# An attention-and-MLP kernel: ScalarE's evacuation of the product with V moves behind the exponential and the high half of its step

## The chip, the core and the metric

The kernel runs on one NeuronCore of a Trainium2 chip. The metric is the device time of one execution in microseconds (us); three runs of the kernel before gave 865.6, 866.25 and 870.39, so the median is 866.25. Engines are called as the profile calls them: PE is TensorE (PEld its weight loads), DVE VectorE, ACT ScalarE, POOL GpSimd, SP SyncE, whose queue issues most of the DMAs.

## What is computed

Attention over 4 batches with 8 heads each, with queries averaged in pairs, followed by a layer norm and a two-layer MLP that is added to its input:

```python
batch, n_heads, seq, head_dim = (4, 8, 1152, 64)
q_pool = q.reshape(B, H, S // factor, factor, D).mean(axis=3)
scores = scale * np.matmul(q_pool, k.transpose(0, 1, 3, 2))
scores = scores - np.max(scores, axis=-1, keepdims=True)
attn = np.exp(scores)
attn = attn / (np.sum(attn, axis=-1, keepdims=True) + 1e-09)
x = heads of np.matmul(attn, v) side by side          # (4, 576, 512)
xn = (x - mu) / np.sqrt(var + 1e-06) * g_ln
out = x + np.maximum(xn @ w_ch1, 0.0) @ w_ch2         # 512 -> 2048 -> 512
```

## The kernel before

The attention is cut into 144 steps. A step is one block of 128 query rows of one pair of heads against all 1152 keys; nine steps make a pair of heads, 36 steps a batch. Products that need more than half precision are made from high and low fp16 halves. The program is one long list written by `step(i)`, and each engine executes its own part of that list strictly in order; nothing reorders it later.

From the second batch on (steps 36 to 143) a step goes through these stations, named by their lines:

- PE writes the scores of step i+1 to PSUM (L362 for the first 1024 keys, L370 for the last 128). The scores of a step fill a slot of three PSUM banks; even and odd steps use two slots in turn. Scores take only the first 128 columns of the slot's third bank, and columns 128 to 257 of that bank hold the product with V of an earlier step.
- DVE finds the row maximum (L381, `mx`) and scales it (L386, `nb`). ACT computes the exponential (L395, `pe`) and its fp16 high half (L409, `hl`). DVE, or in three steps of nine POOL (L251, L416), makes the low half (L418), and SP issues the DMA that transposes both halves (L421, `pt`). Three `hl` buffers are in turn.
- Four steps later PE multiplies the transposed block with V (`emit_pv`, L464, 27 short accumulations in a row); this is called a piece. Its evacuation has two parts (`evac_pv`): `one` on DVE adds a small number to the row sums and inverts them (L513, L514, `r`), `two` on ACT scales the 64 result columns by `r` into `xb` (L524; `xh` for the fifth step of a pair, as two instructions).
- `evacuated` then counts, and when the eight heads of 128 rows are complete it queues a layer norm: DVE takes statistics (L550, L551), POOL normalizes (L556 to L562), PE transposes (L568).
- Between the steps PE runs units of the MLP (L605 the first layer, L637 the second), as a rule one per step, and preparations of the next pair (L297, L301, L325 transposes of k and q). A unit or preparation takes one of two remaining PSUM banks, and must be evacuated before the bank is written again: units by ACT L618 and DVE L619 (`ht`) or DVE L650, preparations by ACT L286 or L311 and DVE L283 or L306. ACT also computes sums of absolute values for the scales of a pair (L185), which PE transposes (L201).

The order around the change: evacuations are collected in the list `evacs`, in the order of their matmuls: first the piece, then the unit, then the preparation, all of them issued at the end of step i-1. `flush()` in step i runs the list: it stands after the scores of step i+1, behind the maximum of step i on DVE and ahead of the exponential of step i on ACT. A unit can also call `flush()` in its middle, so that in some steps the list runs at the step's end.

Of the kernel before, what the change touches and what calls it, by code (L numbers as in the profile page):

```python
# [24 lines left out]
def tile_pooled_attention_moe(  # L25
# [310 lines left out]
    def on_pe(i):  # L336

        return 0 <= i < HP * C
# [67 lines left out]
    def emit_hi(i):  # L406
        st = steps[i]
        hl = st["hl"] = p_p.tile([128, 2, S], FP16, tag="hl", name="hl", bufs=3)
        nc.scalar.activation(out=hl[:, 0], in_=st["pe"], func=ACTF.Copy, scale=2.0 ** 15)  # L409
# [21 lines left out]
    def emit_t_copy(i):  # L431
        st = steps[i]
        for a, b in ((0, 512), (512, S)):
            nc.scalar.copy(st["pt"][:, a:b], st["s"][:, a:b])

    def emit_pv(i, ps=None):

        p, j = divmod(i, C)
        b, hp = divmod(p, HP)
        vt, pt = pair[p]["v"], pts.pop(i)  # L440
        if ps is None:
            ps = psum[:, 3 * (pv_slot[0] % 2) + 2, 128:258]
        if j == 4:
            o = 64 * (b % 2)
            parts = [(h, 64 * h, 64, ps[o:o + 64, 65 * h:65 * h + 65]) for h in range(2)]
        else:
            parts = [(PLACES[p % HP // 2][j][0], 0, 128, ps[:, 0:65])]
        if on_pe(i):
            pt = pt.rearrange("p a n -> p (a n)").bitcast(FP32)
            for h, q0, w, _ in parts:  # L450
                for u, c in enumerate(ORDER):
                    nc.tensor.matmul(  # L452
                        out=ps[0:65, q0:q0 + w], lhsT=vt[:, h, c],
                        rhs=pt[:, 128 * u + q0:128 * u + q0 + w],
                        start=(u == 0), stop=(u == C - 1),
                    )
            return ps
        for h, q0, w, dst in parts:
            for u, c in enumerate(ORDER):
                x = vt[:, h, c]  # L460
                hi, lo = pt[:, u, q0:q0 + w], pt[:, C + u, q0:q0 + w]
                for lhsT, rhs in ((hi, x[:, 0:65]), (hi, x[:, 66:130]), (lo, x[:, 0:65])):
                    n = rhs.shape[1]
                    nc.tensor.matmul(  # L464
                        out=dst[:, 0:n], lhsT=lhsT, rhs=rhs,
                        start=(u == 0 and lhsT is hi and n == 65),
                        stop=(u == C - 1 and lhsT is lo),
                        skip_group_check=True,
                    )
        return ps  # L470
# [16 lines left out]
    def evac_pv(i, ps):  # L487

        p, j = divmod(i, C)
        b, hp = divmod(p, HP)  # L490
        s = pair[p]["s"][:, 2:3]
        r = sm_p.tile([128, 2], FP32, tag="r", name="r", bufs=3)
        if j == 4:
            if b % 2 == 0 and hp == 0:
                xh[b // 2] = x_p.tile([128, 2, DM], FP32, tag="hh", name="xh")
            o, n, m = 64 * (b % 2), 64, 2
            x = xh[b // 2][o:o + n, 0, 128 * hp:128 * hp + 128]
        else:
            if j == 0 and hp == 0:
                room["x"] -= 4  # L500
                assert room["x"] >= 0
                xb[b] = x_p.tile([128, 4, DM], FP32, tag="xb", name="xb")
            h, t = PLACES[hp // 2][j]
            o, n, m = 0, 128, 1
            x = xb[b][:, t, 128 * hp + 64 * h:128 * hp + 64 * h + 64]
        r = r[o:o + n, 0:m]

        def one():
            sums = ps[o:o + n, 64:65 * m:65]
            if on_pe(i):  # L510
                nc.vector.reciprocal(r, sums)
            else:
                nc.vector.tensor_scalar(r, sums, EPS, s[o:o + n], op0=ALU.add, op1=ALU.mult)  # L513
                nc.vector.reciprocal(r, r)  # L514

        def two():
            for u in range(m):
                if on_pe(i):
                    nc.vector.tensor_scalar(
                        x[:, 64 * u:64 * u + 64], ps[o:o + n, 65 * u:65 * u + 64],  # L520
                        r[:, u:u + 1], None, op0=ALU.mult,
                    )
                    continue
                nc.scalar.activation(  # L524
                    out=x[:, 64 * u:64 * u + 64], in_=ps[o:o + n, 65 * u:65 * u + 64],
                    func=ACTF.Copy, scale=r[:, u:u + 1],
                )

        return one, two
# [7 lines left out]
    def bank():  # L537
        for _ in range(2):
            for _ in free_banks:
                nbank[0] += 1  # L540
                n = nbank[1] = free_banks[nbank[0] % len(free_banks)]
                if n not in held and n not in waiting:
                    waiting.add(n)
                    return psum[:, n]
            flush()
# [31 lines left out]


    units, preps = deque(), deque()
    evacs = []  # L580

    def flush():
        mine, evacs[:] = list(evacs), []
# [333 lines left out]
    def evacuated(n):  # L917

        p, j = divmod(n, C)
        b = p // HP  # L920
        left[p] -= 1
        if not left[p]:
            pair.pop(p)
        key = ("h", b // 2) if j == 4 else (b, PLACES[p % HP // 2][j][1])
        whole[key] = whole.get(key, 0) + 1
        if whole[key] == 8 and key != ("h", 0):
            norms.append(key)
# [7 lines left out]
    def a_prep():  # L935
        if preps:
            fn, p, u = preps.popleft()
            evacs.extend(fn(p, u))
# [6 lines left out]
    def a_piece(i):  # L945
        pieces.extend(ready.pop(i, ()))
        for u in range(2 if len(pieces) > 2 and not on_pe(i) else 1):
            if pieces:
                n = pieces.popleft()
                pt = pts[n]  # L950
                ps = emit_pv(n, bank() if u or on_pe(n) else None)
                if on_pe(n):
                    ot = pt.rearrange("p a n -> p (a n)").bitcast(FP32)[0:65, 0:128]
                    evacs.append(lambda ot=ot, ps=ps: nc.scalar.activation(
                        out=ot, in_=ps[0:65, 0:128], func=ACTF.Identity, bias=eps
                    ))
                    turned.append((n, ot))
                    continue
                evacs.extend(evac_pv(n, ps))
                evacs.append(lambda n=n: evacuated(n))  # L960

    def step(i):
        live = i < NSTEP
        this[0] = i
        for fn, a in early.pop(i, ()):
            fn(*a)
        if live:
            emit_max(i)
        if on_pe(i - 1):
            emit_t_copy(i - 1)  # L970
            steps.pop(i - 1)
        while found:
            found.popleft()()
        first = on_pe(i - 2) or on_pe(i)
        if first and not on_pe(i):
            a_piece(i)
        if on_pe(i):
            if i < 3:
                warm(16, bank())
            a_piece(i)  # L980
            a_prep()
            emit_exp(i)
        while scaled_out:
            scaled_out.popleft()()
        if i + 1 < NSTEP:
            emit_s(i + 1)
            pv_slot[0] = i + 1
        else:
            free_banks[:] = [6, 7, 0, 1, 3, 4]
            pv_slot[0] += 1  # L990
        if on_pe(i):
            while fill:
                drip()
            flush()
        else:
            flush()
            if live:
                emit_exp(i)
                emit_hi(i)
        if 0 <= i - 1 < NSTEP and not on_pe(i - 1):  # L1000
            emit_lo(i - 1)
            steps.pop(i - 1)
            drip()
        norm(i)
        while soon or len(fill) > 3:
            drip()
        if on_pe(i):
            emit_t(i)
            if reds:
                found.append(reds.popleft()())  # L1010
        elif reds:
            evacs.append(reds.popleft()())
        while turned:
            n, ot = turned.popleft()
            emit_turn(n, ot, i)
        if not on_pe(i):
            if not first:
                a_piece(i)
            some_units(i)
            a_prep()  # L1020
        for fn, a in todo.pop(i, ()):
            fn(*a)
        if calm and i < HP * C - 1:
            gate()
        for _ in range(1 if i < HP * C - 1 else 2):
            if calm:
                fn, n = calm.popleft()
                fn(n)
# [6 lines left out]
    with tc.manual_schedule():  # L1035
# [33 lines left out]
        one, two = all_max(st["acc"], 3, lambda ps: scales(0, ps, 0, 3, both=True))  # L1069
# [46 lines left out]
```

## Time and profile before

| | us |
|---|---|
| median of 3 runs | 866.25 |
| the profiled execution, its own time | 860.85 |
| its span on the core | 859.0 |
| PE busy in the span | 810.0 (94%) |
| DVE busy | 604.2 (70%) |
| ACT busy | 561.8 (65%) |
| POOL busy | 349.5 (41%) |

The program has three stages. The first batch takes the time up to about 183 us and treats its pieces in another way (PE transposes them, and DVE scales them in L519, which reads the same 64 columns of the third bank as L524 does later). The second to fourth batch take from 183 to about 735 us. From 735 us to the end the attention is over and PE works off the remaining units. Busy times are shares of the span; the time of an engine between two of its instructions is idle time, and the profile names the event that ended it. Idle time of an engine that is not the bound costs nothing by itself.

### The profile page before, as it was taken

The numbers are of one execution on the slowest core, as the hardware profiler recorded it, in microseconds if no ns is written. First come the engines' busy times: TensorE is split into PE (matmuls) and PEld (weight loads), VectorE is DVE, ScalarE is ACT, GpSimd is POOL, SyncE is SP. The second block draws the span as 40 slices with busy tenths as digits, with TensorE's granted clock in tenths as the row PEclk, the third lists the DMA queues.
The fourth block names the chain that finished last, engine by engine and source line by source line (L and its number), as shares of the span: only waits on it lengthen the run. The fifth ranks groups of instructions, "written<-read, shape, count | busy, mean of one in ns | idle before, by whom it ended". The sixth has DMA issues, their size and how long they took to land.

```text
span 859.0 us, 21617 instructions
## 1 busy us (share of the span) xinstructions
PE 810.0 (94%) x9142; PEld 574.4 (67%) x9142; DVE 604.2 (70%) x1166; ACT 561.8 (65%) x810; POOL 349.5 (41%) x345
## 2 busy tenths in 40 slices
PE   7999999988889998998999999999999999999997
PEld 6787877766556665656575766666666666766764
DVE  4698899898778877788777777777777777531221
ACT  3999988867676767677686867676867676311110
POOL 3020333487888845436534244634542514300000
PEclk9999999999999999999999999999999999999999
DMA  6853465025695869887898989776989968500001
GB/s 178 223 206 122 158 179 182 1 63 107 134 203 110 175 124 223 147 166 141 156 180 158 174 146 203 146 153 123 217 143 158 171 117 139 100 10 20 19 2 24
DMA packets 276016, 115.95 MB, mean 135 GB/s; under 512 B 259280, under 2 KB 259280, under 8 KB 275920
## 3 DMA queue, kind: packets, MB, share of 16 engines
q1 hardware_dynamic: 275568, 113.70, 64.5%
q8 instruction: 71, 1.16, 0.6%
q10 hardware_dynamic: 352, 0.88, 0.4%
q14 instruction: 25, 0.20, 0.1%
HBM read 46.14 MB, written 4.72 MB: 59 GB/s over the span
## 4 chain that ended last, share of the span: by engine, by line
PE 45%; DVE 27%; ACT 12%; DMA 8%; issue 4%; POOL 2%; SPq 2%; ACTq 0%; POOLq 0%; DVEq 0%
PE psum L637 14%; PE psum L605 14%; DVE mx L381 8%; DVE hl L418 6%; PE psum L464 5%; PE psum L362 4%; ACT pe L395 3%; DMA qr<-in_q_dram 2%; DMA kr<-in_k_dram 2%; DVE ht L619 2%; PE psum L452 2%; ACT ht L618 2%; DMA pt<-hl 2%; DVE kt L283 2%; PE psum L428 2%
## 5 line engine op out<-in xcount | busy, mean ns | idle before, releaser
L381 DVE TENSOR_REDUCE mx<-psum 128x1 f32<-128x1152 f32 x144 | 194.7, 1352 | 19.3 <-ACT xb L524 7.4
L637 PE MATMUL psum<-wsl,ht 128*128 128x512 f16 x864 | 196.6, 379 | 5.1 <-DVE ht L619 4.3
L395 ACT ACTIVATE pe<-psum,nb,sc 128x1152 f32<-128x1152 f32 x144 | 188.8, 1311 | 11.8 <-DVE nb L386 10.4
L605 PEld LDWEIGHTS <-wsl 128*128 128x128 f16 x1920 | 170.2, 98 | 28.2 <-issue 9.6
L605 PE MATMUL psum<-xn,wsl 128*128 128x256 f16 x1536 | 178.1, 274 | 8.8 <-DVE xb L650 5.9
L637 PEld LDWEIGHTS <-ht 128*128 128x128 f16 x864 | 80.8, 98 | 93.6 <-issue 5.8
L409 ACT ACTIVATE hl<-pe 128x1152 f16<-128x1152 f32 x108 | 125.6, 1163 | 9.5 <-DMA pt<-hl 6.2
L362 PE MATMUL psum<-kt,qt 64*128 64x512 f16 (+1 forms) x960 | 127.3, 380 | 1.9 <-ACT pe L395 0.9
L619 DVE SCALAR_TENSOR_TENSOR ht<-psum,ht 128x512 f16<-128x512 f32 x72 | 49.8, 692 | 100.7 <-ACT ht L618 100.7
L464 PE MATMUL psum<-vt,pt 128*128 128x65 f16 (+1 forms) x3240 | 118.4, 194 | 0.2 <-DMA pt<-hl 0.2
L418 DVE SCALAR_TENSOR_TENSOR hl<-pe,hl 128x1152 f16<-128x1152 f32 x72 | 112.1, 1556 | 0.0
L464 PEld LDWEIGHTS <-pt 128*128 128x128 f16 (+1 forms) x3240 | 110.1, 101 | 2.8 <-DMA pt<-hl 0.7
L618 ACT ACTIVATE ht<-psum 128x512 f16<-128x512 f32 x72 | 42.7, 593 | 87.0 <-PE psum L605 86.6
L251 POOL TENSOR_SCALAR pe<-pe 128x1152 f32<-128x1152 f32 x36 | 43.1, 1198 | 130.5 <-ACT hl L409 130.5
L524 ACT ACTIVATE xb<-psum,r 128x64 f32<-128x64 f32 x96 | 29.9, 311 | 93.8 <-DVE r L514 80.6
L416 POOL TENSOR_TENSOR hl<-pe,hl 128x1152 f16<-128x1152 f32 x36 | 85.5, 2374 | 3.0
L452 PE MATMUL psum<-pt,vt 128*65 128x128 f32 (+1 forms) x720 | 77.4, 263 | 1.1 <-DVE qt L283 1.1
L452 PEld LDWEIGHTS psum<-pt,vt 128*65 128x65 f32 x720 | 71.5, 138 | 1.3 <-DVE qt L283 1.3
L362 PEld LDWEIGHTS <-qt 64*128 64x128 f16 (+1 forms) x960 | 39.7, 96 | 39.6 <-issue 22.1
L370 PEld LDWEIGHTS <-qt 128*128 128x128 f16 (+1 forms) x320 | 17.0, 99 | 61.5 <-issue 61.4
L283 DVE SCALAR_TENSOR_TENSOR qt<-psum,s,qt 128x384 f16<-128x384 f32 x48 | 29.5, 615 | 31.1 <-ACT qt L286 31.0
L257 POOL COPY gate<-gate 128x1 f32<-128x1 f32 x27 | 5.2, 193 | 110.5 <-DVE gate L256 110.5
(116 smaller groups left out, 1010.8 us busy)
## 6 DMA issues: line engine op xcount, KB each, us to landing
stage<-in_moe_w_ch_dram SPq DMA_DIRECT2D x32, 512.0 KB, 5.9
kr<-in_k_dram SPq DMA_DIRECT2D x16, 576.0 KB, 4.6
qr<-in_q_dram SPq DMA_DIRECT2D x31, 288.0 KB, 6.1
vr<-in_v_dram SPq DMA_DIRECT2D x15, 576.0 KB, 5.0
out_dram<-xb SPq DMA_DIRECT2D x32, 128.0 KB, 2.4
pt<-hl SPq DMA_TRANSPOSE x108, 4.9
kr<-in_k_dram SPq DMA_DIRECT2D x16, 64.0 KB, 4.2
vr<-in_v_dram ACTq DMA_DIRECT2D x1, 576.0 KB, 6.5
```

What stands on the lines that cost most here:

```text
L362: nc.tensor.matmul(out=sp[o:o + w, c0:c0 + 512], lhsT=qt[r:r + 64, qa, q0:q0 + w], rhs=kt[r:r + 64, ka, h], start=(a == 0), stop=(a == 2),)
L381: nc.vector.tensor_reduce(mx, st["s"], axis=AX.X, op=ALU.max)
L395: nc.scalar.activation(out=st["pe"], in_=st["s"], func=ACTF.Exp, scale=pair[i // C]["sc"][:, 0:1], bias=st["nb"],)
L409: nc.scalar.activation(out=hl[:, 0], in_=st["pe"], func=ACTF.Copy, scale=2.0 ** 15)
L416: nc.gpsimd.tensor_tensor(hl[:, 1], st["pe"], hl[:, 0], op=ALU.subtract)
L418: nc.vector.scalar_tensor_tensor(hl[:, 1], st["pe"], 2.0 ** 15, hl[:, 0], op0=ALU.mult, op1=ALU.subtract)
L452: nc.tensor.matmul(out=ps[0:65, q0:q0 + w], lhsT=vt[:, h, c], rhs=pt[:, 128 * u + q0:128 * u + q0 + w], start=(u == 0), stop=(u == C - 1),)
L464: nc.tensor.matmul(out=dst[:, 0:n], lhsT=lhsT, rhs=rhs, start=(u == 0 and lhsT is hi and n == 65), stop=(u == C - 1 and lhsT is lo), skip_ ...
L605: nc.tensor.matmul(out=ps[:, o:o + n], lhsT=wsl[:, 8 * w + cc, wa, f * 128:f * 128 + 128], rhs=xn[:, xa * KD + cc, 0:n], start=(m == 0), s ...
L618: lambda: nc.scalar.activation(out=hi, in_=pv, func=ACTF.Relu),
L619: lambda: nc.vector.scalar_tensor_tensor(lo, pv, 0.0, hi, op0=ALU.max, op1=ALU.subtract),
L637: nc.tensor.matmul(out=ps, lhsT=hv[0][:, ha, f, t * 128:t * 128 + 128], rhs=wsl[:, 8 * w + 4 + f // 2, wa, (f % 2) * DM:(f % 2) * DM + DM] ...
```

## The change

`evac_pv` still returns `one` and `two`, but only `one` goes to `evacs`. `two` and the call of `evacuated` go to a new list, `last`. A step takes what is in `last` when it starts, and runs it behind the exponential and the high half of that step.

```diff
-    evacs = []
+    evacs, last = [], []
...
-                evacs.extend(evac_pv(n, ps))
-                evacs.append(lambda n=n: evacuated(n))
+                one, two = evac_pv(n, ps)
+                evacs.append(one)
+                last.extend((two, lambda n=n: evacuated(n)))
...
         first = on_pe(i - 2) or on_pe(i)
+        final, last[:] = list(last), []
...
             if live:
                 emit_exp(i)
                 emit_hi(i)
+        for fn in final:
+            fn()
```

On ACT, step 60 (about 309 to 314 us in the trace of before), the last rows of step 59 ahead of it. In before:

```order
L395 ACTIVATE pe_4325<-psum_79,nb_4302,sc_3313 128x1152
L409 ACTIVATE hl_4327<-pe_4325 128x1152
L524 ACTIVATE xb_2799<-psum_79,r_4359 128x64
L618 ACTIVATE ht_4100<-psum_79 128x512
L311 ACTIVATE kt_4045<-psum_79,s_4043 128x256
L395 ACTIVATE pe_4410<-psum_79,nb_4392,sc_3313 128x1152
L409 ACTIVATE hl_4412<-pe_4410 128x1152
L524 ACTIVATE xb_2799<-psum_79,r_4445 128x64
```

The same place in the changed kernel:

```order
L395 ACTIVATE pe_4324<-psum_79,nb_4302,sc_3313 128x1152
L409 ACTIVATE hl_4326<-pe_4324 128x1152
L524 ACTIVATE xb_2799<-psum_79,r_4271 128x64
L618 ACTIVATE ht_4100<-psum_79 128x512
L311 ACTIVATE kt_4045<-psum_79,s_4043 128x256
L395 ACTIVATE pe_4409<-psum_79,nb_4392,sc_3313 128x1152
L409 ACTIVATE hl_4411<-pe_4409 128x1152
L524 ACTIVATE xb_2799<-psum_79,r_4359 128x64
```

The kinds of rows stand in the same sequence; what moved is which piece L524 evacuates: `r_4359`, which DVE makes in step 60 after that step's maximum, stands ahead of L618 in before and behind L409 now, and in its old place stands `r_4271` of the step ahead.

On PE, at the scores of a step of the later batches (last score matmuls, as a piece of the difference, with the semaphores waited for):

```order
 L362 MATMUL psum<-kt,qt 128x512
 L370 LDWEIGHTS qt
-L370 MATMUL psum<-kt,qt 128x128
+L370 MATMUL psum<-kt,qt 128x128 [waits Activation_49]
 L370 LDWEIGHTS qt
 L370 MATMUL psum<-kt,qt 128x128
```

No PE row moved; the first matmul into the third bank of a slot now waits for the L524 that last read that bank. This is so in 101 steps; before, it waited for DVE's L513 or for nothing of its own.

On DVE, at the statistics of a layer norm (the step that begins at 390 us in the trace of before):

```order
 L619 SCALAR_TENSOR_TENSOR ht<-psum,ht 128x512 [waits Activation_49]
 L418 SCALAR_TENSOR_TENSOR hl<-pe,hl 128x1152 [waits DMAHW5_49]
-L550 BN_STATS bs<-xb 128x6
+L550 BN_STATS bs<-xb 128x6 [waits Activation_49]
 L551 BN_AGGR mv<-bs 128x2 [waits DVE_49]
 L232 TENSOR_SCALAR red<-psum 128x3 [waits PE_49]
```

No DVE row moved; the statistics now wait for ACT's L524 of their own step. Thirteen layer norms have this new wait, eight of them between 183 and 720 us. The order of POOL's and SP's instructions is that of before.

## Rows read from the trace of the kernel before

**Rows 1.** Two stretches: length, busy us (instructions) by engine, PEclk, DMA share, GB/s

```profile
183.00:735.00 552.00, 518.76 (x6469) 351.93 (x6468) 424.56 (x766) 392.28 (x520) 284.98 (x243) 0.99 0.83 155
735.00:859.00 124.00, 119.29 (x988) 81.28 (x986) 32.26 (x59) 16.83 (x32) 7.83 (x15) 1.00 0.12 25
```

**Rows 2.** Waits of PE, 183 to 735 us: us in total, times, longest us

```profile
PE psum L201 <- ACT kt L185: 7.7, 6, 2.2
PE psum L605 <- DVE xb L650: 5.9, 4, 2.1
PE psum L637 <- DVE ht L619: 4.3, 5, 1.0
PE psum L605 <- DVE ht L619: 2.9, 4, 1.7
...
PE psum L637 <- DVE xb L650: 0.8, 2, 0.6
```

**Rows 3.** Waits of ACT, the same stretch

```profile
ACT xb L524 <- DVE r L514: 69.7, 61, 2.4
...
ACT hl L409 <- DMA pt<-hl: 6.2, 7, 2.8
```

**Rows 4.** Timeline, steps 59 and 60: start us, us, instruction, [idle before <-releaser]

```profile
307.56 2.78 PE L605 MATMUL psum<-xn,wsl 128*128 128x256 f16 x24
...
308.60 1.16 ACT L409 ACTIVATE hl<-pe 128x1152 f16<-128x1152 f32 x1
...
311.25 0.28 PE L370 MATMUL psum<-kt,qt 128*128 128x128 f16 x2
...
311.42 0.16 DVE L514 RECIPROCAL r<-r 128x1 f32<-128x1 f32 x1
311.68 0.32 ACT L524 ACTIVATE xb<-psum,r 128x64 f32<-128x64 f32 x1 [1.92 <-DVE r L514]
311.89 0.59 ACT L618 ACTIVATE ht<-psum 128x512 f16<-128x512 f32 x1
...
312.51 0.69 DVE L619 SCALAR_TENSOR_TENSOR ht<-psum,ht 128x512 f16<-128x512 f32 x1 [0.93 <-ACT ht L618]
312.72 1.32 ACT L395 ACTIVATE pe<-psum,nb,sc 128x1152 f32<-128x1152 f32 x1
...
313.25 2.75 PE L637 MATMUL psum<-wsl,ht 128*128 128x512 f16 x12 [0.91 <-DVE ht L619]
```

**Rows 5.** Timeline, steps 55 and 56

```profile
287.48 0.57 ACT L286 ACTIVATE qt<-psum,s 128x384 f16<-128x384 f32 x1
...
288.09 0.62 DVE L283 SCALAR_TENSOR_TENSOR qt<-psum,s,qt 128x384 f16<-128x384 f32 x1 [0.92 <-ACT qt L286]
...
293.21 2.78 PE L605 MATMUL psum<-xn,wsl 128*128 128x256 f16 x24 [1.90 <-DVE xb L650]
```

**Rows 6.** Timeline: third-bank scores and the high half ahead of them, four places

```profile
194.37 0.27 PE L370 MATMUL psum<-kt,qt 128*128 128x128 f16 x2 [0.28 <-DVE xb L519]
...
240.92 1.16 ACT L409 ACTIVATE hl<-pe 128x1152 f16<-128x1152 f32 x1 [0.96 <-DMA pt<-hl]
...
242.23 0.28 PE L370 MATMUL psum<-kt,qt 128*128 128x128 f16 x2
...
334.39 0.28 PE L370 MATMUL psum<-kt,qt 128*128 128x128 f16 x2
...
334.95 1.16 ACT L409 ACTIVATE hl<-pe 128x1152 f16<-128x1152 f32 x1 [2.83 <-DMA pt<-hl]
...
386.71 1.16 ACT L409 ACTIVATE hl<-pe 128x1152 f16<-128x1152 f32 x1
...
387.50 0.30 PE L370 MATMUL psum<-kt,qt 128*64 128x128 f16 x4
```

**Rows 7.** Timeline: a layer norm's statistics and the high half of their step

```profile
395.16 1.16 ACT L409 ACTIVATE hl<-pe 128x1152 f16<-128x1152 f32 x1
395.52 0.69 DVE L550 BATCH_NORM_STATS2 bs<-xb 128x6 f32<-128x512 f32 x1
```

**Rows 8.** A stretch at the lower clock, columns as in rows 1

```profile
251.28:254.70 3.42, 3.35 (x37) 2.79 (x38) 2.12 (x3) 3.08 (x5) 3.34 (x3) 0.50 1.06 200
```

## The prediction

> **What bounds the kernel now.** I read the stretches first, then PE's waits in the stretch that the change touches, then the timeline around those waits. Between 183 and 735 us PE is busy 518.76 of 552.00 us, so it stands still for 33.2 us; DVE is busy 424.56 and ACT 392.28 us [rows 1]. From 735 us on the timeline shows no idle PE at all. PE's work is the same before and after, so a gain can only come out of those 33.2 us, and whatever shortens ACT's or DVE's chains elsewhere is hidden by PE.
>
> PE's waits name what to look for [rows 2]. The largest, 7.7 us for ACT's sums L185, ends with the landing of k or v in most of its six places. Four groups end with DVE evacuating a PSUM bank that PE wants to write, or a tile that it wants to read: 5.9, 4.3, 2.9 and 0.8 us, 13.9 us in 15 waits. The rest, about 11.6 us, are transitions from the first batch and waits for transposes of x whose chain runs from PE to ACT to DVE and back without the moved instruction.
>
> ACT itself stands still 69.7 us, 61 times, in front of L524, because the reciprocal `r` is not there [rows 3]. That wait looks large beside 33.2 us, but it costs only what of it reaches PE.
>
> **The change, part by part.** Nothing is added or removed. L524 takes the same 0.32 us; ACT's sequence of instructions reads the same, but L524 evacuates the piece of one step earlier, whose `r` is a step old.
>
> *The wait that goes, at its typical place.* In step 60 [rows 4] ACT ends the high half at 308.60 + 1.16 = 309.76 and stands still 1.92 us until `r` (311.42 + 0.16 = 311.58). Only then come L524 and the unit's high half L618 (311.89), though PE's L605 was complete at 307.56 + 2.78 = 310.34. DVE's L619 waits for L618 and starts at 312.51, and PE's L637 waits 0.91 us for L619. With the older piece, L524 runs at 309.8, L618 from 310.4 to 311.0, both beside DVE's maximum. L619 follows L514 directly, at 311.62. It is 312.51 - 311.62 = 0.89 us earlier, and so is L637. The exponential no longer stands behind `r` either: with L618 and the preparation done by 311.5 it starts at about 311.55 instead of 312.72, 1.2 us earlier.
>
> *The same at all places of the four groups.* The five waits of L637 for L619 (4.3 us, longest 1.0) are of this form; each loses 0.89 or its whole length, 4.2 us. Of the four waits of L605 for L619 (2.9 us), the longest, 1.7, keeps 1.7 - 0.9 = 0.8; the others go: 2.1 us. In the four waits of L605 for L650 (5.9 us) the chain is preparation, low half, maximum, L650, back to back on DVE. At two of the four the preparation waits for PE, not for L524, and nothing is gained. At the wait of 1.90 [rows 5] DVE's L283 (288.09) waits for ACT's L286 (287.48), which stands behind an L524 and a high half that move ahead with the exponential. The bounds are 0.1 and 1.2 us (the exponential's gain above); I take 1.0, because every link behind it follows without a pause. The fourth is short and goes: 0.3. The two waits of L637 for L650 (0.8 us) follow a maximum that itself waited for an L524; 0.6 goes. Sum: 4.2 + 2.1 + 1.3 + 0.6 = **8.2 us**.
>
> *The wait that comes, on PE.* L370 of step i+2 now waits until the third bank is read, behind the high half of step i. Queued behind it on PE are the piece, the unit and the preparation. In step 60 the high half ends at 309.76 [rows 4], L524 would follow to 310.1, and L370 starts at 311.25: 1.2 us to spare. Over the 106 such pairs I found six where the high half plus 0.36 us (0.32 and a semaphore) ends after L370. The first is at 242.23, where it ends at 242.08, a cost of 0.2; the last at 387.50, where it ends at 387.87, 0.7; the worst at 334.39, behind a high half that waits 2.83 us for a transposing DMA and ends at 336.11, 2.1 [rows 6]. All six together are 4.4 us at the old times. Most of it disappears: at 387.50 and the two places near 288 the high half moves ahead with its exponential, and at 242 and 334 PE stands still soon after anyway, for L650 [rows 2], so the delay falls into that wait. I leave 0.3 us for 334.39; the bounds are 0 and 4.4.
>
> *The wait that comes, on DVE.* Statistics L550 wait for L524 of their own step. The high half ends at 396.32 [rows 7] and L524 would at 396.65, so L550 moves from 395.52 by 1.1 us, and behind it on DVE stand the next maximum and PE's next evacuations. There are eight such places inside the stretch, 8.8 us of DVE at most. DVE has 127 us idle in the stretch, and PE has work in hand after most of them; the transposes of x behind these rows come some tenths later. I take 0.2, with bounds 0 and 8.8. Where the high half waits for a DMA [rows 3] ahead of sums for L201, L524 adds its length once more: 0.2.
>
> *Sum.* 8.2 - 0.3 - 0.2 - 0.2 = 7.5 us. The profiled execution is 860.85 us (859.0 span, 1.85 around it), so it would take 853.4. It ran 5.4 us below the median of 866.25; taking the same 7.5 us off the median gives 858.75, or **859**. About 0.5% (4.3 us: 861.9 and 870.6) is what a measurement of this kernel can tell from no change.
>
> **The rivals.**
>
> *The gain is taken back at fixed landings.* If the landings of k and v before each L201 did not move ahead with PE, all that is gained ahead of one of them would be waited away there. Then only what lies behind the last of the six counts, some 2.0 us of the 8.2, plus the step before it: 866.25 - 2.5 = 863.75. For it speaks that DMA is busy 0.83 of the stretch [rows 1]; against it, that SP issues the loads at fixed places of the program, so they start earlier too.
>
> *The new wait of L370 decides.* The rows [rows 6] show the mechanism before the change: at 194.37 this matmul waited 0.28 us for DVE's L519, which reads other columns of the same bank. The Trainium skill says the same on its page "PSUM — Partial Sum Buffer", under Terms: no two of TensorE, VectorE and ScalarE may access one bank within a partition at once. By that rule the later read holds up every later score matmul of that bank, and the change would make the loop from exponential to scores longer by high half and L524. In rows of this case that is 1.16 + 0.32 = 1.5 us more in each loop. It costs PE only where L370 comes less than 0.36 us after the high half; if the earlier exponential does not appear, the six places cost 4.4 us with nothing gained: 866.25 + 4.4 = 870.65, slower than before. The point from which it decides is thus a margin of 0.36 us, and [rows 4] have 1.5.
>
> *More than counted.* Two stretches of 3.42 us run at a granted clock of 0.50, 1.2 GHz, each behind two waits of PE of about 2 us; PE was busy 3.35 us in the one shown [rows 8], at the full clock half of that. If a shorter wait keeps the clock up in both, 3.4 us more are gained: 866.25 - 8.2 - 3.4 = 854.65. Against it, those waits are for L650 and L201, which the change hardly moves.
>
> That the change doesn't do what it says I leave at nothing: the order shows the move in every step.
>
> **How the numbers follow.** Forecast (853 to 862 in itself): 0.52. Landings take it back, 862 to 866: 0.24. L370 or the statistics decide, above 866: 0.13, most of it below 870.6. More than counted, below 856: 0.11. The likeliest gives 859. The range reaches down to the case of more, 854, and up to 867.5, which takes in the landings and a net of nothing and leaves out most of the third case. Faster by over 0.5%: 0.52 less a share near the bound, plus 0.11, 0.62; slower by over 0.5%: the upper part of the third case, 0.07; within: 0.31.
>
> **What would show it.** Right: ACT's wait at L524 for `r` falls from 69.7 us to nearly nothing; PE's waits for L619 at L637 and L605 fall from 7.2 to about 1 us; L395 starts about 1 us earlier after its maximum; the waits for L201 stay near 7.7. Wrong: PE waits at L370 for L524 add up to more than 2 us, DVE waits at L550 that are followed by idle PE, or the idle time of PE returns at L201. If PE's idle time in the stretch falls from 33.2 to 26 us and the time does not, the sum was made against the wrong thing.

## The result and the profile after

The changed kernel takes 853.8 us (median of 6 runs, 850.59 to 854.55), the kernel before beside it 864.66 us (6 runs with the three already known, 862.87 to 870.39). The ratio is 0.9862, 95% interval 0.9828 to 0.9896: faster by about 11 us, where 7.25 us were forecast. The measured median lies just under the lower end of the range, 854.0. The profiled execution took 853.66 us, its span 851.5; before it was 860.85 and 859.0. So the two profiles are only 7.2 us apart, and the sum of 7.5 us was made against such a profile. Both differences have to be explained.

The stretches of the changed kernel, columns as in [rows 1]:

```profile
183.00:735.00 552.00, 525.94 (x6563) 356.67 (x6562) 430.73 (x777) 392.05 (x524) 293.81 (x254) 0.99 0.83 157
735.00:851.00 116.00, 111.61 (x903) 76.59 (x901) 29.39 (x51) 15.03 (x28) 1.97 (x7) 0.99 0.10 22
```

PE is busy 525.94 of 552.00 us, so it stands still for 26.1 us in place of the 33.2 of [rows 1]. That is what the prediction named: a fall to 26. The waits of PE in the same stretch (us in total, times, longest us) show where it came from:

```profile
PE psum L201 <- ACT kt L185: 7.1, 5, 2.3
PE psum L568 <- DVE ht L619: 4.6, 4, 1.5
PE psum L370 <- ACT xb L524: 3.2, 3, 1.5
PE psum L568 <- DVE qt L283: 2.8, 2, 1.4
PE psum L605 <- DVE xb L650: 2.5, 2, 1.9
...
PE psum L201 <- POOL rs L556: 0.9, 1, 0.9
PE psum L605 <- DVE ht L619: 0.6, 1, 0.6
```

Against [rows 2]: L637 no longer waits at all (4.3 and 0.8 us before), L605 waits 0.6 us for L619 (2.9 before) and 2.5 for L650 (5.9). L201 waits 7.1 + 0.9 = 8.0 us, about as before (7.7). New are 3.2 us at L370 for L524, in three places. The waits of L568 for L619 only stand in the place of others: all of L568's waits are 7.8 us, 7.4 in before.

The typical place, step 60 (start us, us, instruction, idle before and its releaser), answers to [rows 4]:

```profile
305.25 2.78 PE L605 MATMUL psum<-xn,wsl 128*128 128x256 f16 x24
305.64 1.16 ACT L409 ACTIVATE hl<-pe 128x1152 f16<-128x1152 f32 x1
306.71 0.30 ACT L524 ACTIVATE xb<-psum,r 128x64 f32<-128x64 f32 x1
307.22 1.34 DVE L381 TENSOR_REDUCE mx<-psum 128x1 f32<-128x1152 f32 x1
...
308.07 0.60 ACT L618 ACTIVATE ht<-psum 128x512 f16<-128x512 f32 x1 [1.06 <-PE psum L605]
...
308.98 0.16 DVE L514 RECIPROCAL r<-r 128x1 f32<-128x1 f32 x1
308.98 1.31 ACT L395 ACTIVATE pe<-psum,nb,sc 128x1152 f32<-128x1152 f32 x1
...
309.06 0.67 DVE L619 SCALAR_TENSOR_TENSOR ht<-psum,ht 128x512 f16<-128x512 f32 x1
...
309.88 1.46 PE L637 MATMUL psum<-wsl,ht 128*128 128x512 f16 x6
```

L524 follows the high half without a pause. L618 starts as soon as PE's L605 is complete and no longer stands behind `r`. L619 follows L514 directly, and L637 has no wait, where it had 0.91 us. The exponential starts 308.98 - 308.56 = 0.4 us after the end of the maximum. In before the maximum of this step was

```profile
309.66 1.34 DVE L381 TENSOR_REDUCE mx<-psum 128x1 f32<-128x1152 f32 x1
```

and the exponential started at 312.72 [rows 4], 1.7 us after its end. ACT's waits at L524 for `r` (69.7 us in [rows 3]) are gone from the list of its waits.

### The profile page after: what moved, and what is told of

Read it like the earlier page. It is cut to its first block, busy times and chain, and to the rows that moved or that the text cites. A ratio compares the mean times of both kernels' runs of the same rounds, so it can differ in the third digit from the quotient of the medians.

```text
span 851.5 us, 21644 instructions
## 1 busy us (share of the span) xinstructions
PE 810.1 (95%) x9142; PEld 574.8 (67%) x9142; DVE 606.4 (71%) x1166; ACT 559.0 (66%) x810; POOL 351.4 (41%) x345
## 4 chain that ended last, share of the span: by engine, by line
PE 54%; ACT 11%; DVE 10%; POOL 9%; DMA 8%; issue 5%; SPq 2%; POOLq 0%; ACTq 0%; DVEq 0%
PE psum L605 16%; PE psum L637 16%; PE psum L464 7%; PE psum L362 6%; ACT pe L395 4%; DVE mx L381 3%; DMA qr<-in_q_dram 2%; DMA kr<-in_k_dram 2%; PE psum L452 2%; POOL hl L416 2%; PE psum L370 2%; DMA pt<-hl 2%; PE psum L428 2%; POOL wsl L251 1%; POOL wsl L782 1%
## 5 line engine op out<-in xcount | busy, mean ns | idle before, releaser
L637 PE MATMUL psum<-wsl,ht 128*128 128x512 f16 x864 | 196.6, 379 | 0.0
L605 PEld LDWEIGHTS <-wsl 128*128 128x128 f16 x1920 | 170.5, 99 | 23.2 <-issue 3.9
L605 PE MATMUL psum<-xn,wsl 128*128 128x256 f16 x1536 | 179.6, 276 | 3.2 <-DVE xb L650 2.5
L637 PEld LDWEIGHTS <-ht 128*128 128x128 f16 x864 | 80.5, 98 | 87.7
L409 ACT ACTIVATE hl<-pe 128x1152 f16<-128x1152 f32 x108 | 125.6, 1163 | 11.4 <-DMA pt<-hl 8.2
L618 ACT ACTIVATE ht<-psum 128x512 f16<-128x512 f32 x72 | 42.9, 596 | 134.0 <-PE psum L605 132.0
L464 PE MATMUL psum<-vt,pt 128*128 128x65 f16 (+1 forms) x3240 | 117.1, 193 | 0.3 <-DMA pt<-hl 0.3
L418 DVE SCALAR_TENSOR_TENSOR hl<-pe,hl 128x1152 f16<-128x1152 f32 x72 | 115.0, 1598 | 0.0
L619 DVE SCALAR_TENSOR_TENSOR ht<-psum,ht 128x512 f16<-128x512 f32 x72 | 49.6, 688 | 87.7 <-ACT ht L618 87.7
L464 PEld LDWEIGHTS <-pt 128*128 128x128 f16 (+1 forms) x3240 | 108.9, 100 | 2.8 <-DMA pt<-hl 0.7
L370 PEld LDWEIGHTS <-qt 128*128 128x128 f16 (+1 forms) x320 | 17.4, 99 | 65.0 <-issue 64.9
L650 DVE SCALAR_TENSOR_TENSOR xb<-psum,inv,xb 128x512 f32<-128x512 f32 x32 | 23.9, 747 | 37.1 <-PE psum L637 36.8
L286 ACT ACTIVATE qt<-psum,s 128x384 f16<-128x384 f32 x48 | 27.8, 578 | 33.0 <-PE psum L325 32.9
```

The costliest lines, as they stand in the source:

```text
L418: nc.vector.scalar_tensor_tensor(hl[:, 1], st["pe"], 2.0 ** 15, hl[:, 0], op0=ALU.mult, op1=ALU.subtract)
L464: nc.tensor.matmul(out=dst[:, 0:n], lhsT=lhsT, rhs=rhs, start=(u == 0 and lhsT is hi and n == 65), stop=(u == C - 1 and lhsT is lo), skip_ ...
L605: nc.tensor.matmul(out=ps[:, o:o + n], lhsT=wsl[:, 8 * w + cc, wa, f * 128:f * 128 + 128], rhs=xn[:, xa * KD + cc, 0:n], start=(m == 0), s ...
L619: lambda: nc.vector.scalar_tensor_tensor(lo, pv, 0.0, hi, op0=ALU.max, op1=ALU.subtract),
L637: nc.tensor.matmul(out=ps, lhsT=hv[0][:, ha, f, t * 128:t * 128 + 128], rhs=wsl[:, 8 * w + 4 + f // 2, wa, (f % 2) * DM:(f % 2) * DM + DM] ...
```

## The experiments

The times of all kernels, with the mean granted clock that each execution lists. The last column comes from a fit of straight lines through all these runs, one level for each kernel and one common slope; it gives the level at a clock of 1. The slope is 0.75 us for 0.001 of clock. The +- behind a difference at equal clock is its 95% interval.

| kernel | runs | median us | mean clock | level at clock 1, us |
|---|---|---|---|---|
| before | 57 | 862.24 | 0.9939 | 857.5 |
| the changed kernel | 18 | 851.90 | 0.9935 | 847.5 |
| L524 of its own piece ahead of the exponential | 6 | 850.56 | 0.9947 | 845.8 |
| L524 between exponential and high half | 12 | 849.27 | 0.9956 | 846.1 |
| before, two waits filled | 12 | 863.73 | 0.9939 | 859.4 |
| the changed kernel, two waits filled | 11 | 850.90 | 0.9969 | 848.6 |
| between exponential and high half, three filled | 6 | 849.27 | 0.9967 | 847.1 |
| ahead of the exponential, three filled | 6 | 850.0 | 0.9967 | 847.0 |
| L524 a step later | 4 | 904.77 | 0.9940 | 900.4 |

With the six runs of the first comparison before has 63, from 857.3 to 870.98 us, median 862.4.

### Both kernels once more

No edit. Theory A: the profiled execution of before was a lucky one, and the sum was right between profiles. Theory B: a timed run always takes some us more than a profiled one.

> The kernel before, once more, with a profile of its own. The question is a term of the prediction's sum: the profiled execution of before took 860.85 us, less than all six timed runs of it (862.87 to 870.39), and the prediction carried this distance over to the changed kernel, whose profiled execution (853.66) lies in the middle of its runs. Theory A, the profiled execution of before was a lucky one: its runs scatter because PE's waits at L605, L201 and the two stretches at half clock differ from run to run, and a second profile shows PE idle 35 to 38 us in the second to fourth batch, in place of 33.2, and a time of 862 to 866. Theory B, a constant distance between a profiled and a timed execution: the second profile shows 33 us again and 860 to 861, and the timed median stays 4 to 5 us above. Ratio to before 1.000 by both, within 0.4%.

> The changed kernel once more. By theory A (the sum of 7.5 us was right between profiles, and the timed gain is larger because before's timed runs hold waits that its profile didn't) the profile shows PE idle 25 to 27 us in the second to fourth batch, and the ratio to before is 0.986 to 0.990. If the sum was right against the timed runs too, and the first comparison's ratio of 0.9862 (0.9828 to 0.9896) was at its edge, the ratio comes out at 0.991. PE's waits at L637 for DVE are nothing again, and those at L370 for ACT's L524 3 us.

Measured: before again 862.0 us, ratio 1.0001 (0.9977 to 1.0024); the changed kernel 851.41 us, ratio 0.9893 (0.9872 to 0.9914). PE's waits in the second profile of before:

```profile
PE psum L201 <- ACT kt L185: 7.7, 5, 2.6
PE psum L605 <- DVE xb L650: 5.4, 4, 1.9
PE psum L637 <- DVE ht L619: 4.3, 5, 1.0
...
PE psum L605 <- DVE ht L619: 2.9, 4, 1.7
```

And in the second profile of the changed kernel:

```profile
PE psum L201 <- ACT kt L185: 5.7, 5, 2.0
PE psum L568 <- DVE ht L619: 4.6, 4, 1.5
PE psum L568 <- DVE qt L283: 2.8, 2, 1.4
PE psum L370 <- ACT xb L524: 2.6, 2, 2.0
PE psum L605 <- DVE xb L650: 1.9, 2, 1.3
```

The waits of L637 and L605 for L619 repeat to the tenth. Those of L605 for L650 vary by some tenths (5.9 and 5.4 us in before, 2.5 and 1.9 in the changed kernel), as does L201, which waits for a chain that often ends with a landing. PE's idle time is 32.4 us in this profile of before and 23.6 in that of the changed kernel. Theory A's 35 to 38 us did not appear, and theory B's constant distance did not either: this profile of before took 859.88 us, 2 us under its median, and that of the changed kernel 851.84, 0.4 above. What goes with the time of a run is the granted clock: over the 57 runs of before it lies between 0.987 (870.98 us) and 1.000 (858.32 us), and the two are correlated with -0.91. Each trace of the two kernels holds a few stretches of 3.41 us at 0.50 (1.2 GHz), their number and places changing from run to run; between 183 and 735 us before had two in both its profiles, at the same places, the changed kernel two in its first and three in its second and third. One such stretch lowers the mean clock by 0.5 x 3.41 / 860 = 0.002, which by the slope is 1.5 us.

The mean clock of the two kernels is the same (0.9939 and 0.9935), so the gain is not the clock's. At equal clock the changed kernel is 10.0 us faster, +-0.6.

### Half of the change

L524 of the step's own piece, behind the evacuations of unit and preparation but ahead of the exponential:

```diff
             flush()
+            for fn in final:
+                fn()
             if live:
                 emit_exp(i)
                 emit_hi(i)
-        for fn in final:
-            fn()
```

> The evacuation L524 of a step's own piece, behind the unit's and the preparation's high halves, but still ahead of the exponential: half of the change. Theory by parts (the prediction): L618 no longer stands behind r, so PE's waits for L619 at L637 and L605 fall from 7.2 to about 1 us as in the changed kernel; the exponential still stands behind r and L524, so the waits of L605 for L650 go back from 2.5 to 4.5 to 6 us; and L370 has no new wait (0.3 us in place of 3.2). Together PE idle 26 to 28 us in the second to fourth batch and a time within 2 us of the changed kernel, ratio to before about 0.987 to 0.990. Rival 1, the exponential's earlier start is what counts: ratio 0.994 or above. Rival 2, the wait of L370 takes back much of the change: this version is faster than the changed kernel by 2 us or more.

Measured: 850.56 us, ratio 0.9869 (0.9837 to 0.9900). PE's waits:

```profile
PE psum L201 <- ACT kt L185: 8.9, 6, 2.1
PE psum L605 <- DVE xb L650: 4.1, 3, 2.0
...
PE psum L568 <- DVE ht L619: 2.1, 2, 1.1
...
PE psum L605 <- DVE ht L619: 0.6, 1, 0.6
```

L637 has no wait, L605 waits 0.6 us for L619, and idle PE is 25.2 us. The parts came out as expected, but for L650 with 4.1 us a little under the 4.5 to 6 and idle PE a little under the 26 to 28, and rival 1 falls: the exponential's earlier start is worth nothing that can be seen. All of the gain comes with the evacuations on ACT (L618, and L286 and L311 of the preparations) no longer behind `r`; no run moves one of these without the others. That includes a place that the prediction put down to the exponential: in step 56, L605 waits 0.58 us for L650 here too, in place of the 1.90 of [rows 5] (0.63 in the changed kernel):

```profile
290.13 1.14 PE L605 MATMUL psum<-xn,wsl 128*128 128x256 f16 x9 [0.58 <-DVE xb L650]
```

In this trace the maximum of step 55 starts at 282.15 and L650 at 289.32, 7.17 us later; before, 285.26 and 292.41, 7.15 us. DVE's chain is not shorter by anything. PE reaches L605 later against it, 7.4 us after that maximum (289.55) in place of 6.05 (291.31), because DVE had fallen less behind in the steps ahead: that maximum waits 0.45 us for PE here, and for nothing in before.

Against the changed kernel this version is 1.6 us faster at equal clock (+-1.1). Rival 2 asked for 2 us, which lies inside this interval, so it is not decided here. The next experiment asks the same in another way.

### L524 between the exponential and the high half

```diff
             if live:
                 emit_exp(i)
+            for fn in final:
+                fn()
+            if live:
                 emit_hi(i)
-        for fn in final:
-            fn()
```

> The same change, but the evacuation L524 of the older piece stands between the exponential and the high half, 1.16 us earlier than in the changed kernel. If the new wait of L370 (3.2 us in three places: 1.12, 1.50, 0.56) is a real cost, it falls to 0.5 us or less, and PE idle falls from 26.1 to about 23.5 us; if L370's wait only takes the place of a wait that stands behind it (L201 in the same step, 1.99 us, and in the next, 2.26 us), PE idle stays at 25 to 26 us and the time within 0.7 us of the changed kernel. DVE's waits at L550 for L524 fall from 9.3 to about 1 us by both. Against it: the high half and with it the low half and the transposing DMA come 0.32 us later, which should cost nothing, since a piece is taken up four steps later. A third possibility: one of the two stretches at half clock behind these waits goes (1.7 us more).

> The changed kernel a third time, beside the three below on one chip. Its 12 runs so far have a median of 851.9 and before's 29 of the last comparison 861.8; by the sum of the prediction (7.5 us) the ratio is 0.991, by the medians so far 0.987 to 0.989. If the idle time of PE is what the time goes by, the profile shows 24 to 26 us of it between the maxima of steps 36 and 143, and the stretch 538 to 539 us long.

> L524 between the exponential and the high half, once more. In the first profile its PE idle time (24.95 us) equals the changed kernel's (26.06 and 23.61), though L370 no longer waits; its timed median (849.3) lay 2 us lower than the changed kernel's (851.4). If the profiles tell it, the two medians of this comparison lie within 1 us of each other; if L370's wait is a real cost of 2 to 3 us, this one is lower by 2 us or more again.

Measured: 849.27 us, ratio 0.9872 (0.9845 to 0.9898); again 849.37, 0.9856 (0.9826 to 0.9886), with the changed kernel beside it at 852.41, 0.9897 (0.9871 to 0.9923). L370 no longer waits for L524, and DVE's wait at L550 falls from 9.3 us (nine times) to 1.4 (three times); the changed kernel first, then this version:

```profile
DVE bs L550 <- ACT xb L524: 9.3, 9, 1.9
```

```profile
DVE bs L550 <- ACT xb L524: 1.4, 3, 0.7
```

Yet PE is idle 24.95 us in this profile, where the changed kernel had 26.1 and 23.6. Step 65 shows why. In the changed kernel:

```profile
330.27 0.82 PE L362 MATMUL psum<-kt,qt 64*128 64x512 f16 x6
331.17 1.16 ACT L409 ACTIVATE hl<-pe 128x1152 f16<-128x1152 f32 x1 [2.42 <-DMA pt<-hl]
332.24 0.30 ACT L524 ACTIVATE xb<-psum,r 128x64 f32<-128x64 f32 x1
332.59 0.27 PE L370 MATMUL psum<-kt,qt 128*128 128x128 f16 x2 [1.50 <-ACT xb L524]
332.70 0.98 PE L464 MATMUL psum<-vt,pt 128*128 128x65 f16 x27
333.51 2.78 PE L605 MATMUL psum<-xn,wsl 128*128 128x256 f16 x24
```

The same place with L524 ahead of the high half:

```profile
329.32 0.28 PE L370 MATMUL psum<-kt,qt 128*128 128x128 f16 x2
329.90 0.99 PE L464 MATMUL psum<-vt,pt 128*128 128x65 f16 x27 [0.29 <-DMA pt<-hl]
332.48 2.78 PE L605 MATMUL psum<-xn,wsl 128*128 128x256 f16 x24 [1.58 <-DVE xb L650]
```

The wait at L370 is gone, and the 1.58 us for L650 that before had at this place (1.61) is back. L370's wait had only taken its place, as the prediction said of 334.39. So part of the fall of L605's wait for L650 in the changed kernel, from 5.9 to 2.5 us, is this exchange. By the medians of the second comparison the two versions are 3.0 us apart (849.37 and 852.41), which is the second of the two cases set, 2 us or more. But the mean clock there was 0.9957 against 0.9923, and over all runs they are 1.4 us apart at equal clock (+-0.9), between the two cases: a little of L370's wait is a cost, more than the idle time of the profiles shows (24.95 and 24.5 us here) and less than the 3.2 us. The statistics' wait costs nothing that can be seen: 8 us less of it moved no idle time of PE.

### The bank held for a step longer

The older piece's L524 stands behind the next step's evacuations and ahead of its exponential:

```diff
-        final, last[:] = list(last), []
+        final, older[:], last[:] = list(older), list(last), []
...
             flush()
+            for fn in final:
+                fn()
             if live:
                 emit_exp(i)
                 emit_hi(i)
-        for fn in final:
-            fn()
```

> L524 of the older piece a whole step later than in the half change: behind the next step's unit and preparation, ahead of the next exponential. The score matmuls L370 no longer meet it; the next piece's L464, which writes the same columns of the same bank, does. This puts a price on the prediction's second rival (a bank that is held longer): at step 60 PE comes to L464 at about 311.6 us by the rows of before, and L524 would end there at about 311.8. If holding the bank past PE's arrival costs what it delays, at most of 106 steps by 0.2 to 0.5 us, PE's waits at L464 for L524 add up to 10 to 40 us and the time is 860 to 885. If PE's waits only trade places, as at L370, the time stays within 3 us of the changed kernel.

Measured: 904.77 us, ratio 1.0503 (1.0474 to 1.0531), outside both expectations. PE's waits from 183 to 770 us:

```profile
PE psum L464 <- ACT xb L524: 28.6, 70, 0.5
PE psum L201 <- ACT xb L524: 9.7, 10, 2.0
PE psum L464 <- ACT xh L524: 6.6, 11, 0.6
PE psum L212 <- ACT xb L524: 3.6, 9, 0.4
```

One step of it, on PE:

```profile
310.24 0.28 PE L370 MATMUL psum<-kt,qt 128*128 128x128 f16 x2
310.93 0.98 PE L464 MATMUL psum<-vt,pt 128*128 128x65 f16 x27 [0.40 <-ACT xb L524]
```

and L524 between them on ACT:

```profile
310.56 0.31 ACT L524 ACTIVATE xb<-psum,r 128x64 f32<-128x64 f32 x1 [0.23 <-PE psum L370]
```

These four groups are 48.5 us. The 35.2 us at L464 are inside the 10 to 40 expected, but L201 and L212, which write other columns of the same bank, were left out, and the tail behind the last maximum is 8.4 us longer (136.7 against 128.3 us). The form of the wait is the finding: 0.40 us, nearly always the same. L524 in turn waits for PE's L370, 81 times for `xb` (43.7 us), though L370 writes the first 128 columns of the bank and L524 reads from column 128 on. L464 must wait in any case: it writes the very columns that L524 reads. So within one step the bank goes from PE to ACT and back to PE, and PE loses 0.40 us, 0.31 of it the read itself, wherever the order of the program puts L524 between L370 and L464. That a later read of the bank holds up PE, as the second rival of the prediction has it, is thus real and dear, though it is L464 and L201 that wait here and not the scores; what decides is whether the reader of the bank stands between two PE uses that follow each other closely. The Trainium skill's page "PSUM — Partial Sum Buffer", Terms, forbids two engines in one bank at once; the program keeps to that with semaphores, as the 0.23 us of L524 behind L370 show, and no run here leaves them out.

### The waits ahead of the lower clock, filled

24 matmuls of 128x128 that nothing reads, into the columns that L201 writes next, in steps 48 and 66 (22 of them, in steps 48, 66 and 75, in the last two versions):

```diff
             ps = place()
+            if this[0] in FILL:
+                warm(NFILL, ps)
             nc.tensor.transpose(ps[0:n], src, ident)
```

> The changed kernel with 24 more matmuls of 128x128 on PE ahead of L201 in steps 48 and 66, into the columns that L201 writes next; nothing reads them. They fill about 1.3 us of the two waits (2.0 and 2.3 us) that stand just ahead of the two stretches at a granted clock of 0.50. Across before's 29 runs the time rises by 0.77 us for 0.001 of mean clock, about 1.5 us for each such stretch. Theory A: these waits let the clock fall; with them filled the two stretches go, the mean clock rises from 0.994 to 0.997 or more, and the time falls by 2 to 3 us. Theory B: the waits at L605 or L370 one step ahead are enough to let it fall, or it falls whatever PE does: stretches stay at about 251 and 335 to 341 us, and the time is the changed kernel's within 1 us (a loss of up to 1 us where L201's wait is shorter in a run than the filling).

> The changed kernel with the filling, again, beside the one above on one chip. As in its first five runs: 849 to 850.5, mean clock 0.998, no stretch at half clock between 183 and 735 us. If that was luck of the runs, stretches at 250 and 335 us come back and the median is 851.5 to 852.5.

> The kernel before with the same 24 matmuls ahead of L201 in steps 48 and 66 that took both stretches at half clock out of the changed kernel. If these waits let the clock fall in both kernels alike, the two stretches near 251 and 343 us go here too, the mean clock rises from 0.994 to 0.998, and the time falls by 2 to 3 us, to 859 to 860; its distance to the changed kernel with the filling is then the gain of the change with the clock out of the way: 7.5 us by the prediction's sum, 8.3 by PE's idle time between the profiles, 9.9 by the runs set to an equal mean clock. If the changed kernel gains by the clock, before stays at 862 with its stretches.

> L524 between the exponential and the high half, with 22 such matmuls ahead of L201 in steps 48, 66 and 75 (waits of 2.57, 2.12 and 1.42 us without them). If the two gains add up (1.4 us at equal clock for the place of L524, 1.5 us for each of one to three stretches at half clock), 846 to 848; if the place of L524 is worth nothing, as the idle time of PE in the profiles says, 849 to 850.

> Half of the change (L524 of the own piece behind the unit's and the preparation's high halves, ahead of the exponential), with the 22 matmuls in steps 48, 66 and 75. By its six runs at equal clock (about 2 us below the changed kernel's) 845 to 848; by PE's idle time in its profile (25.2 us against 23.6 to 26.1) 849 to 850. If it equals or beats the changed kernel with the filling, the exponential's earlier start is worth nothing, and all of the gain is that L618 no longer stands behind r.

Measured: the changed kernel filled 849.85 us, ratio 0.9864 (0.9839 to 0.9888), and 851.71, 0.9878 (0.9849 to 0.9907); before filled 863.73, 1.0020 (0.9997 to 1.0043); the version with L524 ahead of the high half 849.27, 0.9853 (0.9818 to 0.9887); half of the change 850.0, 0.9856 (0.9824 to 0.9889). In the first profile of the changed kernel the filling (L1040 here; L203 and L373 are L201 and L370) stands inside the wait, and no stretch at 0.50 is left between 183 and 735 us; in the second one is left, at 613 us:

```profile
247.12 0.30 PE L373 MATMUL psum<-kt,qt 128*64 128x128 f16 x4 [0.87 <-ACT xb L527]
247.36 1.51 PE L1040 MATMUL psum<-ident 128*128 128x128 f16 x24
249.41 0.27 PE L203 MATMUL psum<-ident,acc 128*3 128x128 f32 x1 [0.54 <-ACT kt L185]
```

In before the stretches only moved, to 245.16, 292.95 and 528.47 us, and the mean clock stayed at 0.9939. The first of them, columns as in [rows 1]:

```profile
245.16:248.57 3.41, 3.41 (x17) 2.35 (x17) 3.41 (x2) 1.50 (x3) 3.41 (x2) 0.50 1.07 218
```

It begins where a wait ends that the filling does not reach, and the unit behind that wait takes 4.44 us, where the same 24 matmuls take 2.78 at full clock:

```profile
245.16 4.44 PE L608 MATMUL psum<-xn,wsl 128*128 128x256 f16 x24 [2.04 <-DVE xb L653]
249.52 0.84 PE L365 MATMUL psum<-kt,qt 64*64 64x512 f16 x12
```

So theory A holds for the changed kernel's clock (0.9969 against 0.9935 in the mean; 0.9984 in the first five runs, 0.9957 in the six after) and fails for before. Its 2 to 3 us of time did not come: the median fell by 1.0 us, and the second comparison's 851.71 lies in the range set for luck in the first five runs, though the stretches near 250 and 335 us did not come back. The other two versions came out at the 849 to 850 us set for no further gain, not at 846 to 848 and 845 to 848. And the filling has a price of its own: at equal clock it costs the changed kernel 1.1 us (+-0.9) and before 2.0 (+-0.7). In the two filled profiles of the changed kernel a wait of 1.3 to 1.4 us at L201 appears in step 57, where its unfilled ones had none, and that of step 120 is 2.0 us in place of 0.9 to 1.05: some of what is filled at one L201 is waited at a later one. For the question of the change the pair of filled kernels is a second measurement: 10.9 us at equal clock (+-1.0), beside 10.0 of the unfilled ones.

No version here is faster than the changed kernel by more than 3 us; the fastest is L524 between the exponential and the high half, filled or not, at 849.3 us.

## Why the prediction was right, and where not

**The reading of the bound was right.** PE's idle time fell from 33.2 and 32.4 us in the two profiles of before to 26.1, 23.6 and 24.0 in three of the changed kernel, 8.3 us in the mean, where 7.5 were summed. One sentence of that reading was wrong: that a gain can only come out of PE's idle time (see below). And the 69.7 us counted at L524 are those for `xb` alone; `xh` waited another 18.9 us.

**Term by term.** L637 for L619: 4.2 counted, 4.3 measured. L605 for L619: 2.1 and 2.3. L637 for L650: 0.6 and 0.8. L605 for L650 less the new wait of L370: 1.3 - 0.3 = 1.0 counted; measured 5.9 - 2.5 - 3.2 = 0.2 between the first profiles and 5.4 - 1.9 - 2.6 = 0.9 between the second. The net is of the right size, but the two terms apart are not: the first was nearly three times and the second ten times as large as written, since they exchange a wait in step 65. The reason given for 1.0 of it, the exponential's earlier start at step 56, is wrong: with the exponential still behind L524 that wait falls just as far. The statistics (0.2 counted, bound 8.8) cost nothing that can be seen. L201 (0.2 counted) waits 8.0, 6.6 and 8.3 us against 7.7.

**The steps that failed are the base and, after it, the size of the sum.** The prediction took its 7.5 us off the median of three runs, 866.25, and built the range on it too. Those three runs (865.6, 866.25, 870.39) are among the slowest eight of 63; the median of all is 862.4, so the base was 3.8 us too high. The sum was about 2.5 us too small: the gain at equal clock is 10.0 us. In the first comparison alone, where before's median was 864.66, the base makes 1.6 us of the miss and the gain of 10.9 the other 3.4. The profiled 860.85 - 7.5 = 853.35 is within 0.5 us of that comparison's 853.8, but partly by luck: against the median of all 18 runs, 851.9, it is 1.5 us too high. The profile was still the better witness: its clock of 0.996 is close to the mean of before's runs, 0.994. By the slope, 0.002 is 1.5 us, which is the whole distance between 860.85 and 862.4. The clock also says why the first two profiles are only 7.2 us apart: 0.996 against 0.993 is 2.2 us by the slope, and 7.2 + 2.2 = 9.4.

**What the sum lacks.** At equal clock the gain is 10.0 us (+-0.6). PE's idle time gives 8.3, the tail behind the last maximum 0.3 (128.6 against 128.3 us). PE's busy time between the maxima of steps 36 and 143 gives 1.1 more: 547.54 - 33.24 = 514.3 us in before with two stretches at 0.50 inside it, 539.30 - 26.06 = 513.2 in the changed kernel with two. The rows give a reason for it, which no run tests by itself. One matmul of L637 lasts 379 ns by the profile (which models the ends of matmuls):

```profile
L637 PE MATMUL psum<-wsl,ht x576: 376/379/390, 218.9 to 714.1; 128*128 128x512 f16 x192
```

but twelve in a row take 2.75 us [rows 4], one each 0.216 us: each starts 0.16 us before the one ahead of it has ended. Ahead of a wait this overlap is lost, and the profile counts that as busy time. All seven waits of L637 are gone, an estimated 7 x 0.16 = 1.1 us; over all of PE the waits listed fall from 35 to 26. The prediction put this term at nothing by calling PE's work the same. The three parts are 9.7 us together.

**The rivals.** *Taken back at fixed landings*: fallen as the answer to the whole change, since PE's idle time fell and L201 did not rise. It is there in small: L201's waits in steps 84 and 120 were 0.35 and 0.51 us in the first profile of before and 0.33 to 1.25 and 0.88 to 1.05 in three of the changed kernel. *L370 decides*: fallen for this change, though the sign that was set for it, more than 2 us of waits at L370, appeared in two of three profiles (3.2, 2.6 and 2.0): they mostly replace others and cost some 1.4 us. That a late read of the bank can cost much is shown by the version with L524 a step later, which loses 42 us against before, most of it at L464, whose columns it holds. *More than counted, by the clock*: the time came out where this rival had put it (854.65), but not for its reason. The changed kernel has no fewer stretches at 0.50 in its profiles than before, and the same mean clock (0.9935 against 0.9939).

## What to carry to other kernels

An instruction that waits for a fresh small result costs what stands behind it in its engine's queue: move it behind work that needs nothing from it, and look at what is freed, not at the length of its own wait (88.6 us of such waits here, worth about 10). Sum the waits of one place together, the one that goes and the one that comes, since they trade, and add the overlap that each wait breaks. Take the sum off the profiled execution, with its clock, and treat a median of three runs that is far above it as a draw; the granted clock of each run tells how lucky it was.

## What the runs showed of the hardware

- Stretches at a granted clock of 0.50 last 3.41 us (twice 6.83) in these traces. Those inside the program begin between 0.8 us before and 1.4 us after the end of a wait of PE of 0.6 to 2.9 us; which of such waits have one beside them changes from run to run, and before's runs lie between 0.987 and 1.000 in mean clock. One costs about 1.5 us; the unit in the one shown took 1.7 us longer.
- In this program semaphores make the engines take turns in one PSUM bank, also where they use different columns: L370 waited up to 2.0 us for L524 in the changed kernel, and L524 for L370 81 times in the kernel with L524 a step later. A read of 0.31 us by ACT between two writes of PE that follow each other directly cost PE 0.40 us.
- The same holds between two readers: in the changed kernel the exponential waits for DVE's L513, which reads another column of the bank that the exponential reads. In before the exponential stood behind L524, which waits for `r` and so for L513.

```profile
ACT pe L395 <- DVE r L513: 10.2, 10, 2.2
```

- A wait of PE costs more than its idle time: matmuls of 128x512 lasted 379 ns and started every 216 ns, so 0.16 us of overlap go with it.
